# Linear attention and MLP mixer on one core: key-value products on two halves of the array, group statistics, wider rounding blocks, and the first pass ordered by tables

## The chip, the core and the metric

The kernel runs on one core of one Trainium2 chip. The core has five engines with queues of their own, each in order: TensorE (PE in the profile; PEld is its weight loading), VectorE (DVE), ScalarE (ACT), GpSimd (POOL) and SyncE (SP), whose queue issues nearly all DMA transfers here. The metric is the device time of one execution in microseconds, the median of several runs. 0.2% of it is 1.8 us.

## The reference

All arrays are float32 in shape (batch 8, heads 8, sequence 576, head size 64); the mixer's weights come in as float64.

```python
kv = np.einsum('bhsd,bhse->bhde', k, v)
out = np.einsum('bhsd,bhde->bhse', q, kv)
rms = np.sqrt(np.mean(out * out, axis=-1, keepdims=True) + 1e-06)
x = (out / rms * g_norm)            # then (B,H,S,D) -> (B, S, H*D) = (8, 576, 512)
h = np.maximum(x.transpose(0, 2, 1) @ w_tok1, 0.0) @ w_tok2      # 576 -> 256 -> 576
u = x + h.transpose(0, 2, 1)
h2 = np.maximum(u @ w_ch1, 0.0) @ w_ch2                          # 512 -> 1536 -> 512
return u + h2
```

## The kernel before

**Two passes.** The first pass goes over the batch in four pairs. For each pair it computes the attention, the norm and the token mixing, and stores `u` in DRAM. The second, the channel stage, computes the channel MLP over nine groups of 512 rows with products of sub-blocks (`channel1_once`, `channel2_once`, then `channel1`, `channel2`); the change doesn't touch it. Between them, the last pair's token mixing runs together with the first transposes of `u` (`turn_u`, PSUM tile `ps_ut`).

**Attention of a pair** (`attention`, L306). `side` is the batch item of the pair, `half` four of its eight heads. `kv` (L307) multiplies k and v for two heads at a time, as two 128x128 products over five row blocks: 20 matmul instructions, since a float32 matmul shows as two. Only the two 64x64 blocks on the diagonal belong to heads; VectorE copies the upper one (L316) and ScalarE the lower one into `kvp`, whose other blocks were set to zero once (L915). `attend` (L360) multiplies 256 query rows by `kvp` into the PSUM tile `ps_o`, of which there is one (two banks); `attend_rem` (L372) does the same for the last 64 rows of both items, into `ps_r`, a tile of the same tag, one item on each half of the array's columns. `norm` (L320) squares on ScalarE (L328), multiplies by the gain on VectorE (L329), sums the squares by head (L334), adds epsilon, takes the root on ScalarE (L339) with one correction step on VectorE (L342 to L347), and scales x head by head on ScalarE (L351, eight instructions for 128 rows). Each of the five chunks of a pair has its own chain of these.

**Token mixing of a pair** (`token_mixing`, L387). `h00` to `h11` are the products with `w_tok1` (two items, two blocks of 128 columns) into four PSUM tiles `ps_h`, `hr` the remaining 64 rows and the four relus, `u0` to `u8` the products with `w_tok2` (`ps_u`, the same four banks), each followed by an addition to x on VectorE and, every second time, a store.

**Rounding.** The float64 weights are brought in as pairs of 32-bit words and turned into float32 by `decode` (L149): one scaling on ScalarE (L162), then on VectorE a clamp, a shift, the sign (L166 to L170), the power of two, the lower word and their sum (L176, L178, L118). This is done in blocks of 384 columns for `w_ch1` (16 of them), 512 for `w_ch2` (12), and five blocks for the token weights.

**Order.** Every engine works in the order in which the kernel writes its instructions (`keep_in_program_order`). In the first pass, strings of step names (`first`, `second`, `both`, `last`) give the order; `run` (L890 on) goes through them, puts rounding steps between them by shares, and issues the parts of a norm one, two and three steps after their attend (`due`). `staggered` orders the rounding steps. Loads of k and v for the next pair are issued right after a kv step's copies, loads of q after `attend_rem` and the last attend.

Of the kernel before, what the change touches and what calls it, by code (L numbers as in the profile page):

```python
# [18 lines left out]
def kernel(  # L19
# [54 lines left out]
    def pool(name, bufs, side="left", stack=ctx, **kw):  # L74
# [12 lines left out]
    work = pool("work", 3, "left", left)  # L87
# [20 lines left out]

    now, due = [0], defaultdict(list)
# [39 lines left out]
    def decode(dst, raw):  # L149
# [8 lines left out]
        bits = dst.bitcast(U32)  # L158

# [4 lines left out]
        def upper():  # L164
            hi = raw()[..., 1]
            keep(nc.vector.tensor_scalar(out=dst, in0=dst, scalar1=TOP, scalar2=-TOP,  # L166
                                         op0=ALU.min, op1=ALU.max))
            keep(nc.vector.tensor_scalar(out=bits, in0=bits, scalar1=3, scalar2=None,
                                         op0=ALU.logical_shift_left))
            keep(nc.vector.scalar_tensor_tensor(out=bits, in0=hi, scalar=0x80000000, in1=bits,  # L170
                                                op0=ALU.bitwise_and, op1=ALU.bitwise_or))

        def lower():
            lo = raw()[..., 0]
            part = stage.tile(list(dst.shape), F32, name="part", tag="part", bufs=2)
            keep(nc.vector.tensor_scalar(out=part.bitcast(U32), in0=bits, scalar1=0xFF800000,  # L176
                                         scalar2=None, op0=ALU.bitwise_and))
            keep(nc.vector.scalar_tensor_tensor(out=part, in0=lo, scalar=2.0 ** -52, in1=part,  # L178
                                                op0=ALU.mult, op1=ALU.mult))
            tensor_add(dst, dst, part)  # L180

        return scale, upper, lower
# [4 lines left out]
    def block(n, loads, dst, turn=lambda raw: raw):  # L187

        raw = []

        def fetch():
            raw.append(stage.tile([P, n, 2], U32, name="raw", tag="raw", bufs=6))
            for o, i in loads(raw[0]):
                dma(o, i)

        return (fetch,) + decode(dst, lambda: turn(raw[0]))
# [15 lines left out]
    def get_ch1(c, f):  # L212
        return block(FQ, lambda raw: [(raw, words(moe_w_ch1)[ts(c, P), ts(f, FQ)])],
                     w_ch1[:, 2 * (f // 2) + c // 2, 2 * (f % 2) + c % 2])

    def get_ch2(f):
        a = 2 * (f // NS)
        return block(DM, lambda raw: [(raw, words(moe_w_ch2)[ts(f, P)])],
                     w_ch2[:, a:a + 2, f % NS],
                     lambda raw: raw.rearrange("p (h n) w -> p h n w", h=2))  # L220
# [85 lines left out]
    def attention(pair):  # L306
        def kv(side, half):  # L307
            n = 4 * pair + 2 * side + half
            kk, vv = k_in[n % 4], v_in[n % 4]
            acc = ps["kv"].tile([P, 2, P], F32, name="ps_kv")  # L310
            for i in range(2):
                for j in range(JJ):
                    matmul(acc[:, i], lhsT=kk[:, j, ts(i, P)], rhs=vv[:, j, ts(i, P)],
                                     start=(j == 0), stop=(j == JJ - 1))
            dst = kvp[side][:, 2 * half:2 * half + 2]
            keep(nc.vector.tensor_copy(dst[:HF, :, :D], acc[:HF, :, :D]))  # L316
            copy(dst[HF:, :, D:], acc[HF:, :, D:])
            load(n + 4)

        def norm(o_ps, c, n):  # L320
            o = o_ps.rearrange("p t (h d) -> p (t h) d", d=D)
            x = X[pair, c] = xps[pair % 2].tile([P, n, DM], F32, name="x", tag=f"x{n}",
                                                 bufs=4 if n == 2 else 1)
            x3 = x.rearrange("p t (h d) -> p (t h) d", d=D)
            shape = [P, n * H, 1]

# [723 lines left out]
```

## Time and profile before

| | |
|---|---|
| median of 3 runs | 887.17 us (886.84 to 887.3) |
| profiled execution | 887.92 us, of which the span is 886.0 us |
| granted TensorE clock over the span | 0.975 |
| busy, share of the span | PE 94%, PEld 83%, DVE 81%, ACT 36%, POOL 7% |
| first pass (0 to 262.18 us): busy | PE 217.20, DVE 189.88, ACT 127.93 us |
| chain that ended last, by engine | PE 80%, DVE 10%, DMA 4%, ACT 4% |

The profile is that of one execution. A group's row gives line, engine, operation, target and sources, shapes and count, then busy time, the mean in ns of one, and the engine's idle time just before with what ended it. Matmul durations hold the way through the array, so the distance between starts is the better measure. A line can be that of a helper (L127 is every matmul, L118 every addition), so the names of the tiles tell the groups apart.

### The profile page before, as it was taken

Reading aid. Unit: us, or ns where it says so; the run is one execution under the profiler, and the core shown is the slowest. Engines: PE = TensorE matmul, PEld = TensorE weight load, DVE = VectorE, ACT = ScalarE, POOL = GpSimd, SP = SyncE. Lnnn points to the kernel's source line nnn. Section 1 sums busy time; section 2 is a strip of 40 time slices with the busy share of each in tenths; the row PEclk is TensorE's granted clock in tenths of the full one; section 3 lists DMA queues with packets and bytes.
Section 4 is the critical chain, followed back from the end, with each engine's and each line's share of the span. In section 5 each row is a group of like instructions: output and inputs, shape, how many; then the busy total and the mean of one; then the engine's idle time right before and its main releaser. Section 6 shows DMA issues by size and latency. Waiting matters only on the chain.

```text
span 886.0 us, 16016 instructions
## 1 busy us (share of the span) xinstructions
PE 833.2 (94%) x6144; PEld 738.4 (83%) x6144; DVE 717.6 (81%) x1442; ACT 316.8 (36%) x892; POOL 61.1 (7%) x46
## 2 busy tenths in 40 slices
PE   5569798997999999999999999999999999999997
PEld 5346455564448889999999999999999999999997
DVE  1476887898877779797798798798798799799796
ACT  1456546644512102432432332332332332342231
POOL 1000000000000000300300300300300300200200
PEclk9688999898999999999999999999999999999999
DMA  9994686731333445444644644644554654654633
GB/s 281 314 325 135 223 280 218 253 127 72 107 121 139 178 166 203 152 139 138 223 155 134 227 158 133 211 157 150 190 171 136 200 182 132 205 178 136 202 120 93
DMA packets 67068, 156.53 MB, mean 177 GB/s; under 512 B 5424, under 2 KB 23856, under 8 KB 66992
## 3 DMA queue, kind: packets, MB, share of 16 engines
q1 hardware_dynamic: 65312, 153.77, 53.1%
q10 hardware_dynamic: 1680, 1.74, 0.7%
q8 instruction: 49, 0.80, 0.4%
q14 instruction: 27, 0.22, 0.1%
HBM read 128.35 MB, written 27.13 MB: 175 GB/s over the span
## 4 chain that ended last, share of the span: by engine, by line
PE 80%; DVE 10%; DMA 4%; ACT 4%; issue 1%; SPq 0%; ACTq 0%; DVEq 0%
PE ps_a L127 33%; PE ps_b L127 16%; PE ps_c L127 8%; PE ps_h L127 5%; PE ps_u L127 5%; PE ps_v L127 4%; PE ps_w L127 3%; DMA v_in<-in_v_dram 2%; ACT x L351 2%; PE ps_ut L454 2%; PE ps_kv L127 2%; PE ps_o L127 1%; DMA raw<-in_moe_w_tok_dram 1%; DVE x L329 1%; DVE sv L118 1%
## 5 line engine op out<-in xcount | busy, mean ns | idle before, releaser
L124 ACT COPY u<-ps_a 128x128 f32<-128x128 f32 (+1 forms) x176 | 60.3, 343 | 176.8 <-PE ps_a L127 164.9
L118 POOL TENSOR_TENSOR v<-v,v 128x768 f32<-128x768 f32 x32 | 58.4, 1857 | 781.9 <-ACT t L124 781.8
L127 PE MATMUL ps_b<-uT,sums 128*128 128x128 f32 x672 | 85.5, 275 | 0.0
L127 PEld LDWEIGHTS ps_b<-uT,sums 128*128 128x128 f32 x672 | 80.2, 192 | 0.0
L127 PE MATMUL ps_a<-uT,w_ch 128*128 128x128 f32 x576 | 78.8, 275 | 0.0
L351 ACT ACTIVATE x<-x,inv 128x64 f32<-128x64 f32 x288 | 70.9, 335 | 16.9 <-DVE inv L347 16.9
L127 PE MATMUL ps_h<-x,w_tok 128*128 128x512 f32 (+1 forms) x160 | 69.3, 626 | 3.9 <-DVE w_tok L118 3.9
L127 PEld LDWEIGHTS ps_a<-uT,w_ch 128*128 128x128 f32 x576 | 71.5, 192 | 0.1
L118 DVE TENSOR_TENSOR v<-ps_b,u 128x384 f32<-128x384 f32 x112 | 60.2, 549 | 12.9 <-PE ps_b L127 12.9
L127 PE MATMUL ps_u<-h,w_tok 128*128 128x512 f32 (+1 forms) x160 | 69.3, 623 | 0.0
L118 DVE TENSOR_TENSOR uT<-uT 128x512 f32<-128x512 f32 (+4 forms) x103 | 63.1, 628 | 2.6 <-ACT uT L124 1.6
L118 DVE TENSOR_TENSOR v<-v,v 128x768 f32<-128x768 f32 (+1 forms) x70 | 64.1, 925 | 0.3
L124 ACT COPY t<-ps_a 128x128 f32<-128x128 f32 (+1 forms) x88 | 30.2, 343 | 92.6 <-PE ps_a L127 85.4
L121 ACT ACTIVATE v<-v 128x384 f32<-128x384 f32 (+1 forms) x102 | 49.4, 526 | 29.2 <-DVE v L118 24.9
L127 PE MATMUL ps_a<-uT,w 128*128 128x128 f32 x432 | 58.7, 275 | 0.0
L127 PEld LDWEIGHTS ps_h<-x,w_tok 128*128 128x128 f32 (+1 forms) x160 | 27.5, 200 | 35.7 <-issue 33.9
L127 PEld LDWEIGHTS ps_u<-h,w_tok 128*128 128x128 f32 (+1 forms) x160 | 26.6, 190 | 32.2 <-issue 29.0
L127 PEld LDWEIGHTS ps_a<-uT,w 128*128 128x128 f32 x432 | 53.4, 192 | 0.0
L127 PEld LDWEIGHTS ps_o<-kvp,qT 128*128 128x128 f32 x256 | 34.7, 213 | 21.8 <-ACT kvp L124 9.1
L118 DVE TENSOR_TENSOR u<-ps_a,v 128x384 f32<-128x384 f32 x48 | 26.8, 558 | 32.1 <-PE ps_a L127 31.6
L127 PEld LDWEIGHTS ps_kv<-v_in,k_in 128*128 128x128 f32 x320 | 39.7, 201 | 15.6 <-DMA v_in<-in_v_dram 6.7
L118 DVE TENSOR_TENSOR xg<-xg,r 128x512 f32<-128x512 f32 (+1 forms) x78 | 50.7, 660 | 0.7 <-ACT r L124 0.6
(119 smaller groups left out, 1703.9 us busy)
## 6 DMA issues: line engine op xcount, KB each, us to landing
sums<-sums SPq DMA_DIRECT2D x112, 576.0 KB, 3.8
qT<-in_q_dram SPq DMA_DIRECT2D x8, 1152.0 KB, 8.1
xt<-u_dram SPq DMA_DIRECT2D x36, 256.0 KB, 3.4
xg<-u_dram SPq DMA_DIRECT2D x18, 512.0 KB, 4.7
k_in<-in_k_dram SPq DMA_DIRECT2D x16, 512.0 KB, 6.3
u_dram<-x SPq DMA_DIRECT2D x16, 512.0 KB, 2.9
out_dram<-xg SPq DMA_DIRECT2D x16, 512.0 KB, 5.5
sums<-sv SPq DMA_DIRECT2D x14, 576.0 KB, 2.8
```

The lines of the kernel that those rows point to most:

```text
L118: keep(engine.tensor_tensor(out=o, in0=a, in1=b, op=op))
L121: keep(nc.scalar.activation(o, a, AF.Relu))
L124: keep(nc.scalar.copy(o, a))
L127: keep(nc.tensor.matmul(*a, **kw))
L329: keep(nc.vector.tensor_mul(x3, o, g_sb.to_broadcast([P, n * H, D])))
L351: keep(nc.scalar.activation(x3[:, i], x3[:, i], AF.Copy, scale=inv[:, i]))
L454: keep(nc.tensor.transpose(pt[:, c], xt[g, i][:, ts(c, P)], ident))
```

## The change

**kv on two halves.** Each head's 64x64 product is now a matmul of its own, and the two heads of a pair of 128 columns use the two column halves of the array, and write the two diagonal blocks of a fixed PSUM tile (`kv_ps[half]`). Its other blocks are set to zero once and stay, so one VectorE copy (`evict`, steps `e00` to `e11`) moves the whole tile. A kv step has 40 matmul instructions of 64 columns instead of 20 of 128.

**Statistics by groups.** Gain (`g`), square (`q`) and the sums (`t`) stay per chunk, gain now before square. Mean (`m`), root (`r`) and inversion (`i`) are done once for a group of chunks: for the first pair (0), (1), (2), (3, 4), for the others (0, 1) and (2, 3, 4), 4 being the remainder. `s30` scales the first 128 rows of chunk 3. The remainder's PSUM tile (`a4`) takes one of the four `ps_h` banks instead of `ps_o`.

**Wider blocks.** `w_ch1` is rounded in 8 blocks of 768 columns, `w_ch2` in 6 of 1024 (two transfers each), `w_tok1` in one of 1024 and one of 256. The six VectorE operations of a block are steps of their own; a scaling is issued six steps ahead, a fetch three blocks ahead; four buffers of raw words instead of six.

**Tables.** `play` goes through the tables `start`, `middle`, `steady` (twice) and `last`; a name with a minus is a step of the attention of the pair before, `l` and `lq` are loads, `w..` steps of token weights (block, then step 0 to 7: fetch, scaling and the six operations), `f` fetches of channel weights, `c` transposes of u, and a number is that many rounding steps (in `last`, with the four sums of `w_ch1` blocks woven in). Of the 85 channel rounding steps, `middle` has 4, each `steady` 26, and `last` 29. At the start the fetches of `w_tok1` now come before the loads of the third and fourth k and v.

```diff
-          for n, b in (("o", 1), ("kv", 2), ("h", 4))}
+          for n, b in (("o", 1), ("kv", 1), ("h", 4))}
...
+        part = []
+        def power():
+            flat = stage.tile([P, 2 * DM], F32, name="part", tag="part", bufs=1)
+            part.append(like(flat[:, :size], dst))
+            keep(nc.vector.tensor_scalar(out=part[0].bitcast(U32), in0=bits, scalar1=0xFF800000,
+                                         scalar2=None, op0=ALU.bitwise_and))
...
     def get_ch1(c, f):
-        return block(FQ, lambda raw: [(raw, words(moe_w_ch1)[ts(c, P), ts(f, FQ)])],
-                     w_ch1[:, 2 * (f // 2) + c // 2, 2 * (f % 2) + c % 2])
+        return block(2 * FQ, lambda raw: [(raw, words(moe_w_ch1)[ts(c, P), ts(f, 2 * FQ)])],
+                     w_ch1[:, 2 * f + c // 2, c % 2:4:2])
...
         def kv(side, half):
             n = 4 * pair + 2 * side + half
             kk, vv = k_in[n % 4], v_in[n % 4]
-            acc = ps["kv"].tile([P, 2, P], F32, name="ps_kv")
             for i in range(2):
                 for j in range(JJ):
-                    matmul(acc[:, i], lhsT=kk[:, j, ts(i, P)], rhs=vv[:, j, ts(i, P)],
-                                     start=(j == 0), stop=(j == JJ - 1))
-            dst = kvp[side][:, 2 * half:2 * half + 2]
-            keep(nc.vector.tensor_copy(dst[:HF, :, :D], acc[:HF, :, :D]))
-            copy(dst[HF:, :, D:], acc[HF:, :, D:])
-            load(n + 4)
+                    for h in range(2):
+                        r = ds(h * D, D)
+                        matmul(kv_ps[half][r, i, r], lhsT=kk[:, j, ds(i * P + h * D, D)],
+                               rhs=vv[:, j, ds(i * P + h * D, D)],
+                               start=(j == 0), stop=(j == JJ - 1), skip_group_check=True)
+        def evict(side, half):
+            keep(nc.vector.tensor_copy(kvp[side][:, 2 * half:2 * half + 2], kv_ps[half]))
...
         def attend_rem():
-            o = ps["o"].tile([P, 1, DM], F32, name="ps_r", tag="o")
+            o = ps["h"].tile([P, DM], F32, name="ps_r", tag="h")
...
+        def gain(c):
...
+            keep(nc.vector.tensor_mul(heads(x), heads(bank[c]),
+                                      g_sb.to_broadcast([P, number(c), D])))
+        def square(c):
+            sq[c] = work.tile([P, number(c), D], F32, name="sq", tag="sq", bufs=1)
+            keep(nc.scalar.activation(sq[c], heads(bank[c]), AF.Square))
...
+    def stream(blocks, ahead=3):
+        steps = [blocks[0][1]]
+        for n, block in enumerate(blocks):
+            steps += block[2:]
+            for at, m, k in ((-6, n + 1, 1), (-1, n + ahead, 0)):
+                if m < len(blocks):
+                    steps[at] = do(lambda *fs: [f() for f in fs], steps[at], blocks[m][k])
+        return iter(steps)
+
+    def play(lines, after={}, **stages):
+        for name in " ".join(lines).split():
+            if name.isdigit():
+                for _ in range(int(name)):
+                    next(stages["rounding"], lambda: None)()
+            elif name[0] == "-":
+                stages["before"][name[1:]]()
+            else:
+                next(stages[s][name] for s in ("attention", "mixing", "more")
+                     if name in stages.get(s, ()))()
...
     load_q(0)
...
+    for block in tok1:
+        block[0]()
     for n in range(2, 4):
         load(n)
     load_q(1)
...
+    start = [
+        "kv00 e00 l00", "kv01 e01 l01", "a0 g0 q0 t0 m0 r0", "a1 g1 q1 i0 t1 m1 w01 w11 r1 s00 i1",
+        "s01 w02 w03 w04", "kv10 e10 s10 w05 w06 w07 w12", "kv11 e11 s11 w13 w14 w15 w16 w17", "h00 w21",
+        "a2 g2 q2 t2 w31 w22 w23", "h01", "a3 g3 m2 q3 r2 t3 i2 w24", "a4 g4 s20 q4 t4 m3 lq0 l10 l11 lq1",
+        "r3 s21 i3"]
+    middle = [
+        "kv00 e00 l00 -s30 -s31", "kv01 e01 l01 -s40 w25 w26 w27 w32", "h10", "h11 w33 w34 w35 w36 w37", "hr",
+        "a0 g0 q0 t0", "u0", "u1", "a1 g1 q1 t1 m0", "u2 r0 i0 f0 f1", "kv10 e10 s00", "u3 s01",
+        "kv11 e11 s10", "u4 s11 f2", "a2 g2 q2", "u5 t2", "a4 g4 q4 lq0 l10 l11", "u6 t4", "a3 g3 q3 lq1", "u7 t3 1",
+        "u8 m2 r2 3"]
+    steady = [
+        "kv00 l00 e00 1 -i2", "h00 1 -s20 -s21 2", "kv01 l01 e01 1", "h01 3 -s30 -s31", "a0 -s40 g0",
+        "h10 1 q0 t0 2", "h11 4", "hr 2", "a1 1 g1", "kv10 l10 q1 e10", "u0 t1 m0", "kv11 l11 r0 e11",
+        "u1 i0 1", "u2 s00 1", "a2 g2", "u3 q2 t2 s01", "u4 s10 1", "a4 g4 lq0", "u5 q4 t4 1", "a3 g3 lq1",
+        "u6 q3 t3 s11", "u7 2", "u8 m2 r2 2"]
...
+    last = [
+        "-i2 h00 2 -s20 -s21 1 c0", "h01 4 -s30 -s31 c1", "h10 -s40 4 c2", "h11 4 c3", "hr 2 c4",
+        "u0 2", "u1 2", "u2 2", "u3 2", "u4 2", "u5 2", "u6 2", "u7 2", "u8"]
```

More of the change, by code (lines that the diff above doesn't have):

```diff
@@ L1 @@
+import math
 from collections import defaultdict
@@ L173, in lower @@
-        def lower():
[L174 to L180, printed above, removed]
```

227 lines of the change are left out of this document (113 added, 114 removed).

## The prediction

> **What bounds the kernel now.** I read the page first, then the busy time by stages, then the chain of waits. From the page: the length, and the slices of TensorE and of its granted clock.
>
> ```profile
> span 886.0 us, 16016 instructions
> ...
> PE   5569798997999999999999999999999999999997
> ...
> PEclk9688999898999999999999999999999999999999
> ```
>
> TensorE is full and at full clock from the twelfth slice on; all gaps lie in the first 262 us, where the change is. The stages below are cut where the matmuls of a pair's first kv step begin (113.72, 170.96), where the last pair's mixing begins (228.71) and where the channel stage begins (262.18). Columns: stretch, length, busy time and instructions of PE, PEld, DVE, ACT, POOL, granted clock, DMA share, GB/s.
>
> ```profile
> 0.00:113.72 113.72, 80.27 (x401) 56.36 (x401) 68.07 (x151) 55.87 (x176) 2.75 (x14) 0.86 0.85 258
> 113.72:170.96 57.24, 51.58 (x242) 31.42 (x240) 45.40 (x105) 31.29 (x99) 0.00 (x0) 0.94 0.71 237
> 170.96:228.71 57.75, 51.87 (x242) 31.47 (x241) 49.36 (x101) 31.83 (x99) 0.00 (x0) 0.94 0.37 130
> 228.71:262.18 33.47, 33.47 (x99) 14.91 (x97) 27.04 (x45) 8.93 (x25) 0.00 (x0) 1.00 0.25 87
> ```
>
> I call these the opening, two steady rounds, and the tail. The chain of waits inside the first steady round (start, length, what):
>
> ```profile
> 154.58 1.03 ACT sq L328
> 155.63 1.23 DVE x L329
> 156.91 1.98 PE ps_r L127 x16
> 158.89 5.06 PE ps_u L127 x8
> ```
>
> The single `ps_o` tile is full; its square waits on ScalarE behind head scalings, the gain on VectorE waits for the square, and the remainder rows (`ps_r`) wait for the tile. The whole pass pays that way: the row of `x<-ps_o` further down has 29.5 us in which VectorE waited for squares.
>
> What full TensorE would need for the round: 57.24, less a wait of 5.0 before `ps_r`, less what the half clock after it costs (8 `ps_u` matmuls took 5.06; eight at full clock take 3.44, below; `ps_r` 1.0), less 0.7 before an attend: **49.0**.
>
> **The kv step.** Before: 20 full-array instructions; the row is 2.23, 0.111 each for 128 columns. After: 40 matmul instructions of 64 columns in pairs on two column halves, with 40 weight loads.
>
> ```profile
> 100.43 1.98 PE ps_r L127 x16
> ...
> 119.65 2.23 PE ps_kv L127 x20
> ```
> ```profile
> 240.59 3.44 PE ps_h L127 x8
> 244.03 0.44 PE ps_ut L454 x4
> 244.47 1.92 PE ps_h L127 x8
> 246.38 15.80 PE ps_u L127 x40
> ```
> ```profile
> 100.60:100.81 0.21, 0.21 (x4) 0.21 (x6) 0.00 (x0) 0.00 (x0) 0.50 0.00 0
> ```
>
> Do halves overlap? `ps_r` already runs on two column halves: 16 instructions in 1.98 us at a granted clock of 0.50. Eight 512-column instructions at full clock take 3.44, so 128 columns at half clock take 0.215 and 16 in a row 3.4. They overlap. At full clock, 40 `ps_u` instructions (32 whole, 8 on halves) take 15.80; 32 × 0.43 is 13.8, so eight halves take 2.0, not 3.44. And 8 `ps_h` on row halves take 1.92 = 4 × 0.43 + 0.2: entering and leaving the split array costs 0.2. So a kv step is 20 × 0.056 + 0.2 = **1.3** where the pairs overlap fully; shorter it can't be, as the columns still stream. Upper end: every instruction by itself, 80 × 0.055 (four `ps_ut` with their weight loads took 0.44; no row shows TensorE issuing steadily faster) + 0.2 = 4.6. I take 1.3, since rows on both halves overlapped; between lies 2.4 (pairs no faster than one whole matmul). Saved: 0.95 a step, 3.8 a round, floor 45.2.
>
> The Trainium skill (TensorE: Matmul & The Clock Gate, What overlaps and what doesn't) says a weight load overlaps a running matmul only when it goes to other rows of the array, and here all pairs use all 128. The trace disagrees in `ps_r`: were no load hidden, 16 of them would take over 2.6, not 1.98. What it would make of the time is rival B's second case.
>
> **VectorE and ScalarE.** Groups of instructions by shape, 0 to 245 us:
>
> ```profile
> L351 ACT ACTIVATE x<-x,inv 128x64 f32<-128x64 f32 x288 | 70.9, 335 | 16.9 <-DVE inv L347 16.9
> L329 DVE TENSOR_TENSOR x<-ps_o,g_sb 128x1024 f32<-128x1024 f32 x16 | 19.6, 1223 | 31.6 <-ACT sq L328 29.5 <-DMA v_in<-in_v_dram 2.0
> L334 DVE TENSOR_REDUCE ms<-sq 128x16 f32<-128x1024 f32 x16 | 19.2, 1202 | 0.0
> L118 DVE TENSOR_TENSOR x<-ps_u,x 128x512 f32<-128x512 f32 x27 | 17.8, 673 | 1.6 <-PE ps_u L127 1.6
> L170 DVE SCALAR_TENSOR_TENSOR w_ch<-raw,w_ch 128x384 uint32<-128x384 uint32 x16 | 9.0, 559 | 0.6
> L162 ACT ACTIVATE w_ch<-raw 128x512 f32<-128x512 f32 x12 | 8.1, 680 | 0.1
> L170 DVE SCALAR_TENSOR_TENSOR w_ch<-raw,w_ch 128x512 uint32<-128x512 uint32 x11 | 7.6, 693 | 0.4
> L168 DVE TENSOR_SCALAR w_ch<-w_ch 128x384 uint32<-128x384 uint32 x16 | 5.8, 360 | 0.5
> L168 DVE TENSOR_SCALAR w_ch<-w_ch 128x512 uint32<-128x512 uint32 x11 | 4.7, 427 | 0.4
> L316 DVE COPY kvp<-ps_kv 64x128 f32<-64x128 f32 x16 | 4.4, 278 | 14.2 <-PE ps_kv L127 14.2
> L347 DVE RECIPROCAL inv<-root 128x16 f32<-128x16 f32 x16 | 4.0, 253 | 0.6
> ```
>
> Rounding: three operations of the dear kind (559 at 384, 693 at 512: 1.05 ns an element over 157) and three cheap (360, 427: 0.52 over 159) per block. By those slopes a 768 block costs 4.6 against 5.5 for two of 384, a 1024 block 5.8 against 6.7; 15 joins save 14 us of VectorE, all beside TensorE. If the cheap ones ran at the dear rate on the strided target (lower bound 0, upper 0.4 more each) a round would gain 5 us of VectorE; I take 0, as the 512 row is strided already. Groups: inverting 40 sums at once costs 1.3 (two reciprocals of 0.25 to 0.63, from no to full growth with the count; 0.41 taken); five chains a pair become two, 2.4 saved. The eviction becomes one VectorE copy, 0.41 by the 278 and 673 rows, and no ScalarE copy follows.
>
> VectorE per round afterwards: gains 5.6, reductions 5.4, group chains 2.7, evictions 1.6, nine additions 6.0, 26 rounding steps at 0.76 = 19.8: 41 of 45. It fits, but lags: gain before square means that VectorE no longer waits for ScalarE; ScalarE waits for it instead.
>
> **The steady rounds**, queue by queue. VectorE comes out of a round some 4.5 late (the last additions, two rounding steps). Behind that stand `e00`, then `i2`, and ScalarE's `-s20 … -s40` at 2.0 per eight scalings (70.9 / 36). `a0` waits for `e01` (about 1.3), `h10`'s last product for `s31` (about 0.5): 45.2 + 1.3 = **46.5**; the second, with 7 of its steps on 1024 columns, **48**. `a3` doesn't wait: its tile is free some 3 us earlier, since `a4` went to another bank.
>
> **The opening.** Its first part by stages, and the chain:
>
> ```profile
> 0.00:46.89 46.89, 24.32 (x148) 20.84 (x149) 17.74 (x37) 16.25 (x45) 2.75 (x14) 0.84 1.03 297
> ```
>
> ```profile
> 11.05 7.25 DMA v_in<-in_v_dram
> 18.31 11.62 DMA raw<-in_moe_w_tok_dram
> ...
> 71.05 9.86 PE ps_h L127 x24
> ```
>
> The DMA engines are full there. `w_tok1` (1.3 MB) now goes ahead of the third and fourth k and v: at 297 GB/s they land 4.4 later, 22.7 and 27; `kv10` and `kv11` wait for them. But the rounding no longer starts after 30. VectorE's queue from `g1` at 20.7 (1.2, `i0` 1.0, wait and `t1` 2.3, `i1` and waits 1.5, `w02` to `w04` 2.6, `e10` 0.4, `w05` to `w07` 3.1, `w12` 0.3) ends near 32.5; then `h00`, over at 37.5. The chain to `h10` is VectorE (`w13` to `w17` 1.9, `g2`, `t2`, `g3`, `t3` at 1.2 each, two waits for squares 2.0, `i2` 1.1, tok2 steps 1.7, `g4` 0.7; about 50.5) and then ScalarE (`s20`, `q4`, `s21`, `s30`, `s31`: 8.6): 59. With `h11` and `hr`, partly at half clock, 66.6 against 80.9. The loads behind `a4` in SP's queue (`l10`, `l11`, two q) land by 60; `kv10` of the next pair comes at 75. The rest is TensorE's: four attends 7.1, remainder 1.1, two kv 2.6, mixing 15.7, 0.5 of waits: 93.6; 1.4 for what such a walk leaves out: **95**, 18.7 saved.
>
> **The tail** pays. Of 85 rounding steps 29 are left (before: some three blocks of 512), at 0.99 on 1024 columns 28.7; four sums of 1536 columns, 1.77 by the dear slope, 7.1; additions 6.1; `outer_u` 2.8; `i2` 1.3: 46, begun 6 late: VectorE ends 52 after the tail's start. TensorE: `i2` ends at +7.3; no kv or attend stands before `h10` here, and `c1` needs the bank that `c0`'s copy frees, on ScalarE behind `-s20`, `-s21` (4.0) and one block's scaling (1.2 by the 680 row): +13.1, a stall of 5.8. `h10` then ends with `s31`, +17.9; `c2`, `h11`, `c3`, `hr`, relus +25.4; nine `u` 15.7, half clock 1.5: +42.6. Then
>
> ```profile
> ACT r L124 <- DMA u_dram<-x: 18.1, 1, 18.1
> ```
> ```profile
> 262.18 12.93 PE ps_v L127 x59
> ```
> ```profile
> u_dram<-x SPq DMA_DIRECT2D x16, 512.0 KB, 2.9
> ```
>
> the first eviction of the channel stage waits for the last store of x (2.9 after the last addition, and 0.6 for the copy). Four products (32 × 0.219 = 7.0) run ahead; the fifth waits from +49.6 to +55.5: 5.9. Tail 48.5, **15.0 lost**.
>
> **Sum**: −18.7 − 10.7 − 9.7 + 15.0 = −24.1. The profiled execution took 887.92 (1.9 outside its span), the median is 887.17; from the median: **863**.
>
> **Rivals.**
> B, the two weight loads of a pair come one after the other (0.111 a pair, 2.4 a step): for it, loads and matmuls are even today (0.111), and `ps_r` at half clock had time for both; +1.1 on 12 exposed steps, 3 absorbed by VectorE's lag: 873. If no load is hidden at all (3 × 0.056 a pair, 3.6 a step), +2.3 on 12, 8 absorbed: 882.
> C, TensorE's issue decides, on the other side: 80 instructions a step at 0.055 with the 0.2 is 4.6; all 16 steps grow by 3.3. The eight of the rounds cost 26, less 4 that the lag there absorbs; the opening 12 (four in its last part, one ahead of `a0`); the tail returns 3, as VectorE comes out of the rounds in time: 894. The sign turns from about 3.9 a step. For it: no row issues faster steadily; against: `ps_r`'s paired starts, and long matmuls before each step let the queue fill. The Trainium skill (TensorE: Matmul & The Clock Gate, Wait — 56ns, not 53.3ns?) gives about 62 ns a matmul where its sequencer decodes: 2.7 a step by that, near B.
> D, VectorE becomes the bound of the rounds: its 41, 5 if the cheap operations lose their rate, and 6 of waits (`t0` behind `-s40`, `t4` behind `s10`, whose squares ScalarE does late): rounds of 52, tail 3 more: 875. For it: sums of 40 columns come in one piece, late; against: rounding steps stand between square and total.
> E, the tail is covered: its rounding ends with TensorE; 36.5 (33.47 and 3 for `i2`) instead of 48.5: 851.
>
> **Chances**: forecast 0.52 (856 to 869 its own), B 0.14 (of it 0.03 for 882), C 0.07, D 0.15, E 0.12. The range 850 to 878 leaves out C, 882 and the edges. Within 0.2% (1.8 us, what can be told apart here) 0.02; slower 0.07, from C; faster 0.91.
>
> **What would show it.** Right: a kv step of 1.3; rounds of 46 to 48; no wait of `ps_r` for `x`; first `ps_h` near 33; in the tail, `ps_ut` waiting for ScalarE and VectorE busy past the last `ps_u`. Wrong: kv steps over 2, `h10` waiting in the rounds, a tail under 40, or a longer channel stage (623.8 now), which I leave unchanged as none of its code is touched.

## The result, and the profile after

The changed kernel took 862.6 us in the median (861.41 to 863.17, 4 runs), the kernel before 887.0 us on the same chip (885.53 to 887.3, 4 runs). The ratio is 0.9726, with a 95% interval of 0.9709 to 0.9743: 24.4 us faster. The profiled execution took 862.08 us.

The page of the changed kernel: its length, the busy time of each engine, TensorE by slices and its granted clock.

```profile
span 860.3 us, 16434 instructions
...
PE 815.9 (95%) x6464; PEld 719.0 (84%) x6464; DVE 698.9 (81%) x1302; ACT 308.1 (36%) x851; POOL 61.1 (7%) x46
...
PE   4679999998699999999999999999999999999997
...
PEclk9889999999999999999999999999999999999999
```

Busy time by stages, cut at the same events as before: the first kv step of the third and of the fourth pair, the start of the last pair's mixing, and the first product of the channel stage. The fifth stretch reaches from that first product (`ps_v`) to the first matmul into `ps_w`.

```profile
0.00:96.27 96.27, 70.89 (x564) 46.59 (x565) 48.66 (x87) 42.68 (x130) 2.75 (x14) 0.93 0.80 256
96.27:142.56 46.29, 45.98 (x326) 25.99 (x323) 39.82 (x61) 29.40 (x89) 0.00 (x0) 1.00 0.99 321
142.56:188.46 45.90, 45.90 (x323) 25.83 (x319) 38.55 (x59) 28.29 (x87) 0.00 (x0) 1.00 0.50 170
188.46:226.77 38.31, 34.22 (x99) 14.60 (x97) 37.65 (x47) 18.44 (x53) 0.00 (x0) 1.00 0.42 144
226.77:272.78 46.01, 39.21 (x171) 33.75 (x170) 35.79 (x55) 7.33 (x12) 0.00 (x0) 0.93 0.38 140
```

In the second steady round TensorE is busy for the whole 45.90 us; in the first for 45.98 of 46.29. Nothing is left to hide there. The loss sits in the last two rows: the tail is 38.3 us where it was 33.5, and the stretch behind it, 46.0 here, was 36.3 before (262.18 to 298.48). Everything after the first `ps_w` matmul lasts 587.5 us in both kernels.

| stage, us | before | forecast | after | change forecast | change measured |
|---|---|---|---|---|---|
| opening | 113.7 | 95 | 96.3 | -18.7 | -17.5 |
| first steady round | 57.2 | 46.5 | 46.3 | -10.7 | -11.0 |
| second steady round | 57.8 | 48 | 45.9 | -9.7 | -11.8 |
| tail, TensorE's own | 33.5 | 42.6 | 38.3 | +9.1 | +4.8 |
| wait in the channel stage's first products | 0 | 5.9 | 9.7 | +5.9 | +9.7 |
| sum | | | | -24.1 | -25.7 |

The measured column is that of the two profiled executions, whose spans are 886.0 and 860.3 us; the medians differ by 24.4.

The kv step, from the chain of waits of the changed kernel (start, length, what):

```profile
142.66 1.17 PE ps_kv L127 x40
143.83 3.63 PE ps_h L127 x8
147.46 1.32 PE ps_kv L127 x40
```

Forty matmuls and as many weight loads pass in 1.17 to 1.32 us, against 2.23 for the 20 of before. The eight `ps_h` matmuls behind them take 3.63 us, 0.19 more than the 3.44 that eight such matmuls took behind a whole-array step in the kernel before.

The waits of the changed kernel up to 226.7 us (who waits, for whom: total, times, longest):

```profile
ACT sq L383 <- DVE x L378: 43.5, 12, 11.6
...
DVE ms L398 <- ACT sq L383: 17.9, 15, 3.6
...
PE ps_h L127 <- DVE w_tok L118: 7.9, 1, 7.9
...
PE ps_ut L506 <- ACT uT L124: 2.0, 1, 2.0
```

VectorE's gains no longer wait for the squares, which cost them 38.2 us in the first pass of before; ScalarE waits for the gains instead, 43.5 us in all. VectorE's sums (`ms`) still wait for squares, 17.9 us. In the two steady rounds none of this holds TensorE up: its only wait there is 0.3 us. No `ps_r` waits for `x`.

The place that costs most now: TensorE and VectorE around the end of the tail (start, length, what, and in brackets the idle time before it and what ended it).

```profile
226.72 1.99 PE L127 MATMUL ps_v<-uT,w_ch 128*128 128x256 f32 x8
235.52 3.78 PE L127 MATMUL ps_v<-uT,w 128*128 128x256 f32 x8 [6.80 <-DVE x L118]
```
```profile
231.38 0.68 DVE L118 TENSOR_TENSOR x<-ps_u,x 128x512 f32<-128x512 f32 x1
...
234.78 0.68 DVE L118 TENSOR_TENSOR x<-ps_u,x 128x512 f32<-128x512 f32 x1
```
```profile
228.81 0.59 ACT L124 COPY r<-ps_v 128x512 f32<-128x512 f32 x1 [15.84 <-PE ps_v L127]
```

The first product ends at 228.7 and its eviction on ScalarE runs at once. The second product waits until 235.5, when VectorE has finished the addition of `u8` (234.78 + 0.68), the last one of the tail. TensorE had written that `u8` by 226.8: VectorE, busy for 37.65 of the tail's 38.31 us, is 8 us behind with it. The products after the pause run at a lower granted clock (0.50 from 235.52 to 239.10 us, where eight matmuls take 3.78 instead of 1.99; 0.70 up to 242.00; 1.00 from there on), so a pause of 6.8 costs 9.7.

### The profile page after: what moved, and what is told of

It is laid out like the page before. It is cut to its first block, busy times and chain, and to the rows that moved or that the text cites. A ratio compares the mean times of both kernels' runs of the same rounds, so it can differ in the third digit from the quotient of the medians.

```text
span 860.3 us, 16434 instructions
## 1 busy us (share of the span) xinstructions
PE 815.9 (95%) x6464; PEld 719.0 (84%) x6464; DVE 698.9 (81%) x1302; ACT 308.1 (36%) x851; POOL 61.1 (7%) x46
## 3 DMA queue, kind: packets, MB, share of 16 engines
q1 hardware_dynamic: 65680, 153.77, 54.4%
## 4 chain that ended last, share of the span: by engine, by line
PE 80%; DVE 13%; ACT 3%; DMA 2%; issue 1%; DVEq 0%; ACTq 0%
PE ps_a L127 34%; PE ps_b L127 17%; PE ps_c L127 8%; PE ps_h L127 5%; PE ps_v L127 4%; PE ps_u L127 4%; PE ps_o L127 3%; PE ps_w L127 3%; ACT x L422 2%; PE ps_ut L506 2%; DVE w_ch L118 1%; DMA qT<-in_q_dram 1%; DVE ms L398 1%; DVE uT L118 1%; DVE part L187 1%
## 5 line engine op out<-in xcount | busy, mean ns | idle before, releaser
L127 PE MATMUL ps_h<-x,w_tok 128*128 128x512 f32 (+1 forms) x160 | 71.4, 636 | 15.4 <-DVE w_tok L118 7.9
L127 PE MATMUL ps_u<-h,w_tok 128*128 128x512 f32 (+1 forms) x160 | 66.5, 601 | 0.6 <-DVE x L118 0.6
L121 ACT ACTIVATE v<-v 128x384 f32<-128x384 f32 (+1 forms) x102 | 49.4, 526 | 40.5 <-DVE v L118 36.3
L127 PEld LDWEIGHTS ps_u<-h,w_tok 128*128 128x128 f32 (+1 forms) x160 | 24.8, 179 | 29.7 <-issue 24.4
L127 PE MATMUL ps_a<-uT,sums 128*128 128x128 f32 x336 | 46.9, 276 | 1.3 <-ACT t L124 1.3
L127 PE MATMUL ps_a<-sums,sv 128*128 128x128 f32 x336 | 47.2, 277 | 0.9 <-ACT r L124 0.5
```

The lines of the kernel that those rows point to most:

```text
L121: keep(nc.scalar.activation(o, a, AF.Relu))
L127: keep(nc.tensor.matmul(*a, **kw))
```

## The experiments

Each was timed beside the kernel before, on its own chip; the ratio is to the kernel before. Stages in us from the profiled execution. "First products" is the stretch from the first `ps_v` to the first `ps_w`.

| kernel | median | ratio, 95% interval | opening | rounds | tail | first products |
|---|---|---|---|---|---|---|
| after | 862.6 | 0.9726 (0.9709 to 0.9743) | 96.3 | 46.3, 45.9 | 38.3 | 46.0 |
| after again | 860.83 | 0.9709 (0.9692 to 0.9725) | 94.9 | 46.3, 45.8 | 38.3 | 46.3 |
| whole-array kv | 866.86 | 0.9775 (0.9745 to 0.9804) | 97.1 | 48.9, 49.0 | 38.3 | 46.0 |
| square first | 865.72 | 0.977 (0.9744 to 0.9796) | 94.2 | 48.7, 47.2 | 40.0 | 45.6 |
| halved rounding steps | 858.05 | 0.967 (0.9646 to 0.9693) | 96.1 | 46.4, 45.8 | 38.3 | 42.8 |
| chains by chunk | 857.57 | 0.9671 (0.9653 to 0.9689) | 94.9 | 45.8, 45.8 | 40.1 | 41.7 |
| `w_tok1` fetched later | 865.38 | 0.9756 (0.9739 to 0.9773) | 99.6 | 46.3, 45.8 | 38.3 | 46.3 |
| remainder in `ps_o` | 865.7 | 0.9764 (0.9744 to 0.9783) | 99.1 | 46.5, 46.6 | 37.7 | 45.6 |
| additions first | 855.13 | 0.9654 (0.9624 to 0.9684) | 95.8 | 46.3, 45.8 | 38.3 | 40.2 |
| rounding earlier | 873.06 | 0.9849 (0.9824 to 0.9874) | 105.3 | 54.4, 47.6 | 39.4 | 36.4 |
| first transpose in `ps_h` | 861.97 | 0.9716 (0.9701 to 0.973) | 95.7 | 46.3, 45.8 | 39.6 | 45.4 |
| additions first, fuller round | 852.49 | 0.9606 (0.9592 to 0.962) | 94.9 | 46.3, 45.8 | 38.8 | 36.4 |
| and later transposes | 854.61 | 0.9632 (0.9618 to 0.9646) | 97.1 | 46.3, 45.8 | 38.9 | 37.6 |

**After again.** The changed kernel once more, beside the last three kernels of the table, on their chip.

> The changed kernel once more, on the chip of the three others, as what they are compared with: 861 to 864 us. The differences of the earlier experiments rest on the ratio to the kernel before; the chips may differ by some 2 us.

It gives the scatter. The opening of kernels that don't touch it lies between 94.9 and 97.1: the first attend starts between 13.7 and 14.6 us, when the first q has landed, and the second attend takes between 2.07 and 3.80; why it does isn't shown. The other stages repeat within 0.3. Differences of a stage beyond these are taken as real below. This chip is also that of "whole-array kv", "square first", "additions first" and "rounding earlier", so 860.83 is the time to compare these with; the other four of the first eight ran on another chip.

**Whole-array kv.** The matmuls of the step go back to 20 on the whole array, with two copies of the diagonal; all else stays.

```diff
-                    for h in range(2):
-                        r = ds(h * D, D)
-                        matmul(kv_ps[half][r, i, r], lhsT=kk[:, j, ds(i * P + h * D, D)],
-                               rhs=vv[:, j, ds(i * P + h * D, D)],
...
+                    matmul(kv_ps[half][:, i], lhsT=kk[:, j, ts(i, P)], rhs=vv[:, j, ts(i, P)],
+                           start=(j == 0), stop=(j == JJ - 1))
...
+            keep(nc.vector.tensor_copy(dst[:HF, :, :D], kv_ps[half][:HF, :, :D]))
+            keep(nc.vector.tensor_copy(dst[HF:, :, D:], kv_ps[half][HF:, :, D:]))
```

> The changed kernel with the kv products back on the whole array (20 instructions of 128 columns a step, two VectorE copies of the diagonal blocks, 0.28 us each, instead of one of 0.41). Theory (the rounds are bound by TensorE, kv lies on its path): a kv step takes 2.2 instead of 1.3 to 1.4 us, 12 of the 16 steps lie on the path, 1 to 3 us are absorbed by waits that get shorter; 870 to 874 us. Rival (the gain comes from the order of the work, the rounds wait for VectorE or ScalarE): within 3 us of the changed kernel.

Stages of this kernel, the two rounds, and its kv step in the chain:

```profile
97.10:146.00 48.90, 48.90 (x242) 30.00 (x240) 39.98 (x65) 28.79 (x88) 0.00 (x0) 1.00 0.93 306
146.00:194.97 48.97, 48.97 (x242) 30.02 (x240) 39.68 (x63) 28.20 (x87) 0.00 (x0) 1.00 0.43 155
```
```profile
103.01 2.23 PE ps_kv L127 x20
```

The step is 2.23 again, and a round 2.6 and 3.1 us longer. By the kv rows alone, four steps would lose 3.6 to 4.2 (0.9 to 1.1 each); the matmuls behind each step, which take 0.19 longer after a split step, account for the rest. The whole came to 866.9, less than the 870 to 874 expected: the opening, 97.1, shows little of its eight steps (its first four are among those that wait for k and v anyway), so it is the rounds that tell. The two halves are worth 4.3 us of the change's 24.4 by the first timing, and 6.0 by the changed kernel's time on the same chip, while the two rounds alone give 5.7. The four runs scatter from 863.85 to 868.54, so this is some 4 to 6 us; the rest comes from elsewhere.

**Square first.** In the tables each square stands before its gain, as in the kernel before.

```diff
-        "kv00 l00 e00 1 -i2", "h00 1 -s20 -s21 2", "kv01 l01 e01 1", "h01 3 -s30 -s31", "a0 -s40 g0",
-        "h10 1 q0 t0 2", "h11 4", "hr 2", "a1 1 g1", "kv10 l10 q1 e10", "u0 t1 m0", "kv11 l11 r0 e11",
...
+        "kv00 l00 e00 1 -i2", "h00 1 -s20 -s21 2", "kv01 l01 e01 1", "h01 3 -s30 -s31", "a0 -s40 q0 g0",
+        "h10 1 t0 2", "h11 4", "hr 2", "a1 1 q1 g1", "kv10 l10 e10", "u0 t1 m0", "kv11 l11 r0 e11",
```

> The changed kernel with the square ahead of the gain again, both where the gain stood, so that VectorE waits for ScalarE. Theory (VectorE's waits for squares were what held the PSUM tile and the rounds before): VectorE idles 1.0 us more per gain, 5 us a pair; the rounds have 6 us of VectorE idle time but the lag moves into the group chains, so 1 to 3 us a round and 4 in the opening: 868 to 873 us. Rival (VectorE has time for it): within 2 us of the changed kernel.

Its waits from 94 to 231 us:

```profile
DVE x L378 <- ACT sq L383: 18.0, 8, 6.2
...
PE ps_ut L506 <- ACT uT L124: 3.7, 1, 3.7
```

VectorE's gains wait for squares again, 18.0 us, where in the changed kernel its sums wait 8.8 from 96 us to the end of the tail, and the rounds are 2.4 and 1.3 longer, the tail 1.7: its first bank of transposes waits 3.7 instead of 2.0. The median, 865.7, is less than expected: VectorE lost some 9 us more to squares, not 18, and had 6 to spare in each round. It is 4.9 us above the changed kernel on the same chip.

**Remainder in `ps_o`.** The remainder rows go back to the tile of the attends.

```diff
-            o = ps["h"].tile([P, DM], F32, name="ps_r", tag="h")
-            bank[4] = o.rearrange("p (t e) -> p t e", t=1)
+            bank[4] = ps["o"].tile([P, 1, DM], F32, name="ps_r", tag="o")
+            o = bank[4][:, 0]
```

> The changed kernel with the remainder's products in the one ps_o tile again instead of a ps_h bank. Theory (the single ps_o tile was what TensorE waited for before): the remainder waits for the square of chunk 2 and the last attend for the square of the remainder, which stands behind scalings on ScalarE: 2 to 3 us a round, 868 to 872 us. Rival (the changed order alone removed that wait): within 1 us.

Its waits up to 192 us:

```profile
PE ps_r L127 <- ACT sq L383: 5.0, 2, 2.6
```

This was a miss. A round was expected to lose 2 to 3 us and lost 0.2 and 0.7: both waits of `ps_r` are over before the rounds begin, and the opening, 99.1, pays for them. In the rounds `ps_r` doesn't wait for the tile, so the move to another bank isn't what removed the 5 us wait there; the order of the rest is enough.

**`w_tok1` fetched later.** The fetch goes back behind the loads of the third and fourth k and v and of the second q.

```diff
-    for block in tok1:
-        block[0]()
...
+    for block in tok1:
+        block[0]()
```

> The changed kernel with the fetch of the first token weights behind the loads of the third and fourth k and v and the second q, as before. Theory (the opening's chain goes through the rounding of these weights): they land near 30 instead of 18 us, ScalarE and VectorE wait for them, the first mixing product starts 3 to 5 us later: 865 to 867 us. Rival (the DMA engines are full either way, k and v come earlier): within 1 us or faster.

From the waits of TensorE up to 50 us:

```profile
PE ps_h L127 <- DVE w_tok L118: 11.7, 1, 11.7
```

The changed kernel's row, among its waits above, has 7.9. `h00` waits 3.8 us longer for the rounding of `w_tok1`, and the opening ends at 99.6, 3.3 later than in the changed kernel's first profile and 2.5 later than the latest of the scatter. 3 to 5 were expected.

**Chains by chunk.** Mean, root and inversion are done chunk by chunk again, in the places of the groups.

```diff
-            ms, root, inv = stat[g]
-            keep(nc.vector.reciprocal(inv, root))
...
+            for c in g:
+                ms, root, inv = stats_of(c)
+                keep(nc.vector.reciprocal(inv, root))
...
```

> The changed kernel with mean, root and inversion done chunk by chunk, in the places of the group's. Theory: VectorE has 2.4 us a pair more, and the inversion of the last group ends 1 to 2 us later, which the first product of the second item sees only in the tail: 863 to 866 us. Rival (the group chain is on the path of every round): 3 to 4 us a pair, 872 us.

**Halved rounding steps.** Each step of a wide block is issued as two instructions of half the width.

```diff
+    def decode_halves(dst, raw):
...
+        parts = [decode(cut(dst, i), lambda i=i: cut(raw(), i)) for i in range(2)]
+        return tuple(do(lambda *fs: [f() for f in fs], a, b) for a, b in zip(*parts))
...
-        return (fetch,) + decode(dst, turn)
+        return (fetch,) + (decode_halves if n > S else decode)(dst, turn)
```

> The changed kernel in which every step of a block of 768 or 1024 columns is done as two instructions of half the width, in the same places of the tables. Theory (wider blocks save 0.95 us of VectorE a block, 14 in all; the rounds have room for it, the tail has not): the rounds stay within 1 us, the tail with its five blocks is 4 to 5 us longer: 866 to 869 us. Rival A (VectorE bounds the rounds): 874 to 878 us. Rival B (no matter): within 1 us.

Both were to be slower and came out faster, by 4.6 and 5.0 us by the medians, or by some 3.5 when their ratios are compared with that of "after again". The steady rounds from 96 to 142 and 142 to 188 us: the changed kernel, then the chains by chunk, then the halved steps.

```profile
96.00:142.00 46.00, 45.69 (x320) 25.85 (x318) 39.41 (x60) 29.67 (x90) 0.00 (x0) 1.00 0.99 320
142.00:188.00 46.00, 46.00 (x324) 25.99 (x320) 38.62 (x60) 28.29 (x87) 0.00 (x0) 1.00 0.51 174
```
```profile
96.00:142.00 46.00, 46.00 (x329) 26.09 (x323) 40.99 (x77) 28.96 (x91) 0.00 (x0) 1.00 1.01 328
142.00:188.00 46.00, 46.00 (x286) 25.47 (x285) 40.03 (x74) 28.53 (x90) 0.00 (x0) 1.00 0.45 161
```
```profile
96.00:142.00 46.00, 45.57 (x320) 25.85 (x318) 39.87 (x86) 29.80 (x96) 0.00 (x0) 1.00 1.01 325
142.00:188.00 46.00, 46.00 (x324) 26.05 (x320) 39.30 (x85) 28.51 (x91) 0.00 (x0) 1.00 0.48 172
```

The chains by chunk add 1.6 and 1.4 us of VectorE to a round, and the rounds don't grow: VectorE has 6 us to spare in each. Their tail is 1.8 us longer. The halved steps add only 0.5 and 0.7, for a reason that the last section shows; so this kernel doesn't undo the wide blocks, and what these are worth by themselves stays open.

The gain lies behind the tail. The same place as above, in the kernel with halved steps:

```profile
226.63 1.99 PE L127 MATMUL ps_v<-uT,w_ch 128*128 128x256 f32 x8
232.18 3.78 PE L127 MATMUL ps_v<-uT,w 128*128 128x256 f32 x8 [3.56 <-DVE x L118]
```
```profile
231.44 0.68 DVE L118 TENSOR_TENSOR x<-ps_u,x 128x512 f32<-128x512 f32 x1
...
234.91 0.68 DVE L118 TENSOR_TENSOR x<-ps_u,x 128x512 f32<-128x512 f32 x1
```

VectorE's last two additions come at the same times as in the changed kernel (231.4 and 234.9), but the second product starts with the end of the last but one, `u7` (231.44 + 0.68 = 232.12), and not with that of `u8`. It doesn't need `u8`'s value, then. What it needs is room in PSUM: the kernel closes the pools of the first pass and lays the tiles of the channel stage's products (`ps_v`) over the same banks, and each addition frees the bank that it read. In the changed kernel the second product has to wait for the bank of `u8`, here for that of `u7`. No trace records banks, so this is inferred from the addition that ends the wait. In the chains by chunk the wait is 3.4 us and ends with `u7` as well (231.24 + 0.68). Why these two edits, which touch no PSUM tile, move the second product to another bank isn't known. So 3 to 4 us of these two kernels' gain go with which addition ends the wait, and neither tells what its edit costs.

**Additions first.** In the tail's table the last additions no longer stand behind two rounding steps each; the steps follow after `u8`.

```diff
-        "u0 2", "u1 2", "u2 2", "u3 2", "u4 2", "u5 2", "u6 2", "u7 2", "u8"]
+        "u0 2", "u1 2", "u2 2", "u3 2", "u4", "u5", "u6", "u7", "u8 8"]
```

> The changed kernel with the last eight rounding steps of the tail behind the addition of u8 instead of between the additions u4 to u8. Theory (TensorE's wait of 6.8 us after the first product of the channel stage is for the PSUM bank that the addition of u8 frees): that wait goes, 856 to 859 us. Rival 1 (VectorE's backlog as such decides): no change within 2 us, the wait only moves behind the second product. Rival 2 (the store of x): the store leaves earlier as well, also a gain, but the wait would then be ScalarE's.

Its wait behind the tail:

```profile
PE ps_v L127 <- DVE r L118: 3.5, 1, 3.5
```

The wait for `x` is gone, with no VectorE work taken away. The table's order put the addition late, not the amount alone. What remains, 3.5 us, comes only after five products: it is a wait for the second addition of the channel stage, which now stands behind the eight steps. The median is 7.5 us below the first timing of the changed kernel and 5.7 below the one on the same chip; the first products are 5.8 shorter.

**Rounding earlier.** Sixteen of the tail's 29 steps move to `middle` (ten) and to the steady rounds (three each), with the fetches of three blocks moved ahead.

```diff
-        "kv00 e00 l00 -s30 -s31", "kv01 e01 l01 -s40 w25 w26 w27 w32", "h10", "h11 w33 w34 w35 w36 w37", "hr",
...
+        "kv00 e00 l00 -s30 -s31", "kv01 e01 l01 -s40 f0 f1 w25 w26 w27 w32", "h10", "h11 w33 w34 w35 w36 w37 f2 1", "hr 6",
...
-        "-i2 h00 2 -s20 -s21 1 c0", "h01 4 -s30 -s31 c1", "h10 -s40 4 c2", "h11 4 c3", "hr 2 c4",
+        "-i2 h00 1 -s20 -s21 1 c0", "h01 2 -s30 -s31 c1", "h10 -s40 2 c2", "h11 2 c3", "hr 1 c4",
```

> The changed kernel with 16 of the 29 rounding steps of the tail moved ahead: ten into the middle table, three into each steady round, put where VectorE waits for a square. Theory (the tail is bound by VectorE, the rounds by TensorE with 6 us of VectorE idle): VectorE's work in the tail falls from about 46 to 30 us, the wait of 6.8 us goes, the rounds stay at 46: 853 to 856 us. Rival (VectorE's queue sets the rounds too): each round grows by 2 to 3 us, the middle by as much, and the total stays within 2 us of the changed kernel.

Its waits from 47 to 106 us, and those of SyncE's queue:

```profile
DVE w_ch L166 <- ACT w_ch L163: 14.0, 1, 14.0
ACT w_ch L163 <- DMA raw<-in_moe_w_ch_dram: 12.9, 1, 12.9
```
```profile
SPq L115 <- DVE x L118: 20.0, 2, 14.3
SPq L115 <- PE ps_r L127: 13.6, 1, 13.6
```

The clearest miss: 853 to 856 expected, 873 measured. Behind the tail it did what it should: 36.4 us, no wait. But the fetches stand in SyncE's one queue behind issues that wait for `ps_r` and for an addition, so a rounding step waited 14 us for its words, with the later chunks' sums and gains queued behind it on VectorE. The opening lost some 9 us, the first round 8, the second 1.7. Fetches and steps were moved together, so what the steps alone would have cost there isn't shown. The DMA share of that round is 0.99 in the changed kernel already, so there is little room in it for more fetching.

**First transpose in `ps_h`.** `c0` takes a bank of `ps_h`, so that `c1` needn't wait for `c0`'s copy.

```diff
-    more = {f"c{i}": do(turn, 0, i, u_psum) for i in range(J)}
+    h_psum = lambda: ps["h"].tile([P, NC, P], F32, name="ps_ut", tag="h")
+    more = {f"c{i}": do(turn, 0, i, u_psum if i else h_psum) for i in range(J)}
```

> The changed kernel with the first transpose of the tail in a ps_h bank, so that the second no longer waits for its copy. Theory (the tail ends when VectorE has done the addition of u8, whose PSUM bank the second product of the channel stage needs; the bank is the same here): TensorE's wait of 2.0 us in the tail goes, its wait after the first product grows by as much, total within 1 us of the changed kernel. Rival (TensorE's stalls in the tail add up): 2 us faster.

The waits of TensorE from 187 to 275 us:

```profile
PE ps_v L127 <- DVE x L118: 6.4, 1, 6.4
PE ps_h L127 <- ACT x L422: 2.5, 2, 2.3
```

The wait of `c1` is gone and nothing is gained: `h10` waits for the scalings instead, 2.3 us, and the addition of `u8` ends 47.9 us after the tail's start, against 47.0 in the changed kernel. The second product still waits for it, although the mixing's banks were used once more here. The stall that the prediction gave 5.8 us to is not where the loss is.

**Additions first, fuller round.** As "additions first", with three after `u8` instead of eight; five steps move into the second steady round, whose words are fetched by then.

```diff
+    fuller = [row.replace("h10 1", "h10 4").replace("u3 q2", "u3 1 q2").replace("u6 q3", "u6 1 q3")
+              for row in steady]
...
-        "u0 2", "u1 2", "u2 2", "u3 2", "u4 2", "u5 2", "u6 2", "u7 2", "u8"]
+        "u0 2", "u1 2", "u2 2", "u3 2", "u4", "u5", "u6", "u7", "u8 3"]
```

> The changed kernel with the last additions of the tail ahead of its last rounding steps, and five rounding steps more in the second steady round (where the DMA engines are half idle), five fewer in the tail. Theory: the wait for the bank goes (the experiment with the additions first: 855), and 5 us less of VectorE in the tail take away the backlog of 3.5 us that was left there: 851 to 853 us. Rival (the second round grows by what it takes, as both rounds did when the first was starved of data): 855 to 857.

Its second round and its first products:

```profile
141.20:187.02 45.82, 45.82 (x323) 25.93 (x319) 42.52 (x64) 29.38 (x88) 0.00 (x0) 1.00 0.54 191
...
225.79:262.16 36.37, 36.37 (x171) 32.03 (x170) 31.62 (x49) 7.22 (x12) 0.00 (x0) 1.00 0.47 174
```

VectorE takes 3.9 us more in the second round, and the round stays at 45.8. TensorE is busy for all of the first products' 36.4 us, against 36.3 in the kernel before. 852.5 us: 34.5 below the kernel before and 8.3 below the changed kernel on the same chip. This version is better than both.

**And later transposes.** The same, with each transpose of u about two steps later in the table, and with five rounding steps instead of three behind `u8`.

```diff
-        "-i2 h00 2 -s20 -s21 1 c0", "h01 4 -s30 -s31 c1", "h10 -s40 4 c2", "h11 4 c3", "hr 2 c4",
-        "u0 2", "u1 2", "u2 2", "u3 2", "u4", "u5", "u6", "u7", "u8 3"]
+        "-i2 h00 2 -s20 -s21 1", "h01 4 -s30 -s31", "h10 -s40 3 c0", "h11 4 c1", "hr 2 c2",
+        "u0 2 c3", "u1 1 c4", "u2 2", "u3 2", "u4", "u5", "u6", "u7", "u8 5"]
```

> As the kernel with fuller second round and additions first, and the transposes of the tail two steps later, so that none waits for ScalarE's scalings and no copy of theirs stands before a scaling. Theory: with VectorE no longer the end of the tail, TensorE's own waits there (2.0 for the copy, 1.5 for scalings) count: 1 to 3 us faster than that kernel. Rival (VectorE still decides): no difference.

Waits of TensorE from 187 to 270 us:

```profile
PE ps_h L127 <- ACT x L422: 3.2, 4, 0.9
PE ps_v L127 <- DVE r L118: 0.9, 1, 0.9
```

A miss: 1 to 3 us faster was expected, 2.1 slower came out. Without the transposes between them, the products of `h10` wait for the scalings, four times, 3.2 us, where in the kernel with the fuller round the second transpose waits 2.8; the tail is as long (38.9 against 38.8). What is longer lies elsewhere: the opening, 97.1 against 94.9, which is within its scatter, and the first products, 37.6 against 36.4, where TensorE waits 0.9 for an addition that stands behind two more rounding steps. So this run doesn't show that the later transposes cost anything; it shows that they gain nothing.

## Why the prediction was right, and where it was not

The time (863 forecast, 862.6 measured) and the shape are right: opening and rounds give some 40 us, the tail gives back 15. By its steps:

**kv step: right in its row, 0.2 too cheap with what follows.** 1.3 was taken, 1.17 to 1.32 measured, so the column halves run beside each other, their weight loads too. Rivals B (2.4 or 3.6) and C (4.6) fall with it. The term that was mis-sized is the 0.2 for entering and leaving the split array: leaving it shows in the row behind, 3.63 instead of 3.44, as another 0.19 a step. The Trainium skill (TensorE: Matmul & The Clock Gate, What overlaps and what doesn't) lets a weight load overlap a running matmul only in other rows of the array; these all use the same 128 rows, and the trace goes against the rule. By the 62 ns a matmul that the Trainium skill gives where the sequencer decodes (TensorE: Matmul & The Clock Gate, Wait — 56ns, not 53.3ns?) the 40 would take an estimated 2.5, by the 25 ns that it gives as the least in any case 1.0; the 29 to 33 ns each that were measured go with the second. The forecast of 3.8 a round came out as 2.6 and 3.1, by the whole-array run.

**Opening: right in sum (95, measured 96.3).** Its inner times were late: `h00` ran from 35.4 to 41.1 instead of 32.5 to 37.5, because the second attend's gain started at 24.2 and not at 20.7. In the second profile of the same kernel `h00` began at 33.1, so part of this is scatter. (The terms that the prediction adds up to 32.5 give 33.1.) `h11` and `hr` ended at 69.2 instead of 66.6, and the stage's end was only 1.3 late. That `w_tok1` should go first is shown by its own run (99.6 without it), and the remainder's bank counts here as well (99.1 without it); how the rest of the 17.5 divides between groups, blocks and order isn't shown.

**Steady rounds: right in the first (46.5, measured 46.3), 2.1 too long in the second (48, measured 45.9).** The step that failed there is the surcharge for seven steps on 1024 columns. VectorE's time in the round was given as 41 and was 38.6, and the fuller round shows that 42.5 fits without a cost. D (VectorE as the bound) falls with it. The close agreement of the first round is partly luck: TensorE's own work was taken as 45.2 and is 46.0, for the step's missing 0.2, four times, and the wait before `a0`, taken as 1.3, isn't there; all of TensorE's waits in the round are 0.3, for scalings, a wait that the prediction names with 0.5 but leaves out of its sum. The floor of 49.0 without the halves was right: the whole-array rounds take 48.9 and 49.0, all of it busy. Of the 11 us, the halves account for about 3 and the gain before the square for about 2 by their own runs, the remainder's bank for under 1; the groups gave the rounds nothing, since with chains by chunk they take 45.8. Some 6 us of each round are left to the order of the tables and the wide blocks, which were not tried one by one: that part is argued, not shown. That VectorE would no longer wait for ScalarE was wrong for the sums, but cost TensorE nothing in the rounds.

**Tail, TensorE's own: 42.6 forecast, 38.3 measured.** The failing term is the stall of `c1`: 5.8 forecast, 2.0 measured. ScalarE around it in the changed kernel:

```profile
190.69 1.16 ACT L163 ACTIVATE w_ch<-raw 128x1024 f32<-128x1024 f32 x1
193.49 3.93 ACT L422 ACTIVATE x<-x,inv 128x64 f32<-128x64 f32 x16 [1.64 <-DVE inv L417]
197.33 0.56 ACT L124 COPY uT<-ps_ut 128x512 f32<-128x512 f32 x1
```

The 16 scalings do stand ahead of `c0`'s copy, but `i2` ended 5.0 after the tail's start and not 7.3, and the block's scaling (1.16) ran ahead of them, in time that ScalarE spent waiting, and not behind: 3.5 of the 3.8. VectorE's end came early by as much: 52 after the tail's start by the forecast, 47.0 measured (234.78 + 0.68 less 188.46). E (851, a covered tail) falls: VectorE was busy for all but 0.7 of the tail.

**The wait behind the tail: 5.9 forecast, 9.7 measured, and for another reason.** The prediction had the first eviction wait for the last store of x, and TensorE stop at the fifth product. The eviction ran at once, and TensorE stopped at the second product, for a bank that VectorE's last addition hadn't freed. The common root, VectorE late at the end of the tail, was right in size (9.4 forecast, 8.7 measured), and two errors near 4 us went in opposite directions: 42.6 + 5.9 = 48.5 forecast, 38.3 + 9.7 = 48.0 measured. The agreement of the sum is partly luck. Two of the signs that the prediction named for being wrong did come: the tail, taken as TensorE's own, is 38.3 and so under 40, and the channel stage, which the prediction left unchanged, grew from 623.8 to 633.5 us. What the prediction should have done is to ask of each of the first products which bank it gets and who read that bank last. That the additions stood behind two rounding steps each in the table made the lateness into a wait, as "additions first" shows.

## What to carry to other kernels

Where an engine has slack in one stage and none in the next, move its work by the row of busy times, but only with words that are in the buffer: five steps into the second round were free, sixteen into the stages from `middle` on cost 8 us in the first round and some 9 in the opening, where their fetches stood in a queue behind waits. At the seam between two stages, put the operations that free PSUM banks ahead of those that can wait, and look at the bank that each of the next products gets. A change in another place can alter which of the earlier tiles a product waits for and move the time by 3 to 4 us, as two experiments did here, and an experiment's verdict must be cleared of that.

## What the runs showed of the hardware

**Pairs on column halves** run beside each other with all their loads: 40 matmuls of 64 columns and 40 loads in 1.17 to 1.32 us. Counted together that is 15 to 17 ns an instruction, far below the 0.055 us that the rows of before allowed as a proven rate. Going over to halves and back costs some 0.2 us each time: 1.32 where the columns alone take 1.12 (20 × 0.056), and 3.63 instead of 3.44 for the matmuls behind.

**VectorE overlaps neighbours that don't depend on one another.** The changed kernel's rounding, where each step needs the one before, and the same steps in two halves, where the second half doesn't need the first:

```profile
115.90 0.96 DVE L174 SCALAR_TENSOR_TENSOR w_ch<-raw,w_ch 128x768 uint32<-128x768 uint32 x1
116.89 0.56 DVE L183 TENSOR_SCALAR part<-w_ch 128x768 uint32<-128x768 uint32 x1
```
```profile
115.80 1.02 DVE L174 SCALAR_TENSOR_TENSOR w_ch<-raw,w_ch 128x384 uint32<-128x384 uint32 x2
116.74 0.62 DVE L183 TENSOR_SCALAR part<-w_ch 128x384 uint32<-128x384 uint32 x2
```

A step that depends on its neighbour starts 0.03 after its end, so a wide step takes 0.99. Two independent halves take 0.94 together, start to start, although the mean of one is 0.549. A dependent step of 384 columns took 0.60 in the kernel before. In these rows, then, some 0.13 us of an instruction (0.60 less half of 0.94) is paid only where the next one has to wait for it, and two interleaved narrow steps cost no more than one wide one.
